# Attention output laid out with tokens on partitions, normalised along the free axis, then turned

## The chip, the cores and the metric

The kernel runs on one core of one Trainium2 chip. The metric is the device time of one execution in microseconds (us), the median over several runs. All executions quoted here are of one state (fast), so they may be compared with each other. Engine names are those of the profile: PE is TensorE's matmuls, PEld its weight loads, DVE is VectorE, ACT is ScalarE, POOL is GpSimd. The granted clock is the share of full speed that the profile records for TensorE. To turn a block is to transpose it, which these kernels do on PE.

## The reference

A linear attention with a root-mean-square norm per head, then a feed-forward block with a squared relu:

```python
# q, k, v: (8 batches, 8 heads, 576 tokens, 64), float32
kv  = np.einsum('bhsd,bhse->bhde', k, v)
out = np.einsum('bhsd,bhde->bhse', q, kv)
rms = np.sqrt(np.mean(out * out, axis=-1, keepdims=True) + 1e-06)
attn = out / rms * g_norm                  # g_norm: (64,)
# x: (4608 tokens, 512), heads side by side
h = x @ w_in                               # (512, 2048)
r = np.maximum(h, 0.0)
y = (s * (r * r) + b) @ w_out              # (2048, 512)
```

The weights come as float64, and the kernel rounds them to float32 on the chip.

## The kernel before

There are twelve token tiles of 384 tokens. A tile's attention is made inside the first feed-forward product ("h product") of the tile before it: one step after each of the 16 h products. Tile 0 has nothing to run inside, so its attention runs alone. The attention comes out with features on partitions, one row of 128 features (two heads) at a time, which is just what the h product moves. The sum of squares over a head's 64 features then lies across partitions, so it is made by a product with a block-diagonal matrix of ones. That leaves it repeated on every feature, and root and reciprocal run on 128x384 elements.

```python
def turn(p):                     # q of two heads, features on partitions
    ps = ps_t.tile([P, J, P], FP32, name="qT_ps", tag="t")
    for j in range(J):
        nc.tensor.transpose(ps[:, j, :], q_in[T][:, j, 2 * p : 2 * p + 2, :], ident)
    st["qT"] = attp.tile([P, J, 2, HB], FP32, name="qT", tag="qT")
    nc.vector.tensor_copy(out=st["qT"].rearrange("p j s t -> p j (s t)"), in_=ps)

def product(p):
    st["x"] = ps_x.tile([P, J, 2, HB], FP32, name="x_ps", tag="x")
    for s in range(2):
        nc.tensor.matmul(st["x"][:, :, s, :], lhsT=bd[:, s, p, :],
                         rhs=st["qT"][:, :, s, :], start=True, stop=True)
    st["sq"] = ...
    nc.scalar.activation(st["sq"], st["x"].rearrange("p j s t -> p (j s t)"), AF.Square)

def rms(p):
    ps = ps_t.tile([P, N], FP32, name="ss_ps", tag="t")
    nc.tensor.matmul(ps, lhsT=ones_bd, rhs=st["sq"], start=True, stop=True)
    st["rms"] = ...
    nc.scalar.activation(st["rms"], ps, AF.Sqrt, bias=eps_col, scale=1.0 / D)

def scale(p):
    inv = ...
    nc.vector.reciprocal(inv, st["rms"])
    ...
    nc.vector.scalar_tensor_tensor(xT[T][:, p, :], st["x"]..., g_col, inv, ALU.mult, ALU.mult)

return [(lambda fn=fn, p=p: fn(p)) for p in range(NP) for fn in (turn, product, rms, scale)]

def mm1(T, f):                   # one h product: four matmuls of 384 columns
    ...
    nc.scalar.activation(r, h, AF.Relu)
    nc.vector.tensor_mul(r2, r, r)
    nc.vector.tensor_scalar(out=gT[T, f], in0=r2, scalar1=s_col, scalar2=b_col, ...)

# the program
for step in attention(0):
    step()
...
for T in range(NT):
    ...
    steps = attention(T + 1) if T + 1 < NT else []
    for f in range(FC):          # 16
        if T == 0:
            w_step(f + 2)        # rounds a weight: five DVE, two ACT, two POOL instructions
        mm1(T, f)
        if steps:
            steps[f]()
    ...                          # then the three o products (mm2) of this tile
```

## Time and profile before

The time is 1291 us. What matters of the profile:

| stretch | length, us | what bounds it |
|---|---|---|
| beginning: attention of tile 0 alone | 34.4 | a chain over PE, ACT and DVE, four rows one after another |
| first tile: weights are rounded | about 168 | DVE, busy 97% and 95% of its two parts |
| h stage of a steady tile | 51.06 | PE, with about 3.3 us lost waiting for DVE |
| o stage of a steady tile | 41.2 | PE without a gap |

A line of a timeline reads: start and duration in us, engine, source line, operation, output and inputs, count, and in brackets how long the engine was idle before it and what ended that. Where PE records overlap their neighbours, the true pace is the distance from start to start. The lines of the kernel before stand in the prediction.

### The profile page before, as it was taken

The page shows a single profiled execution, that of the slowest core. Times are in us where ns is not written, and L with a number is a line of the kernel's source. Part 1 is how long each engine was busy: PE and PEld are TensorE (multiplying, and loading weights), DVE is VectorE, ACT ScalarE, POOL GpSimd, SP SyncE. Part 2 cuts the span into 40 slices and gives each one's busy share as a digit, 9 for nine tenths or more (in the row PEclk, how much of TensorE's full clock was granted, in tenths as well). Part 3 has the DMA queues.
Part 4 walks back from the last instruction along what each step waited for, and adds up shares of the span by engine and source line. Part 5 has one row for each costly group of instructions (what it writes and reads, how often), then busy time and mean ns, then how long its engine had stood idle before and what let it go on. Part 6 is the DMA issues. An engine that isn't in the chain of part 4 may idle for free.

```text
span 1289.6 us, 10478 instructions
## 1 busy us (share of the span) xinstructions
PE 1144.8 (89%) x4272; PEld 605.1 (47%) x4272; DVE 499.7 (39%) x700; ACT 206.8 (16%) x397; POOL 89.1 (7%) x72
## 2 busy tenths in 40 slices
PE   3465644899999999999999999999999999999998
PEld 3232411355455455455455454454554554554553
DVE  0499999235035044053053053052153161251220
ACT  0122322021022021021021021020121120120110
POOL 0054456100000000000000000000000000000000
PEclk9998755899999999999999999999999999999999
DMA  9032224300441000000631000001401000000000
GB/s 235 10 93 75 93 98 144 84 9 1 108 114 24 17 9 0 17 9 1 147 74 25 24 1 9 17 0 46 103 1 33 17 1 9 16 1 17 8 1 24
DMA packets 63664, 55.20 MB, mean 43 GB/s; under 512 B 40576, under 2 KB 48768, under 8 KB 63616
## 3 DMA queue, kind: packets, MB, share of 16 engines
q1 hardware_dynamic: 57984, 45.10, 13.6%
q10 hardware_dynamic: 5632, 9.44, 1.9%
q8 instruction: 33, 0.54, 0.2%
q14 instruction: 15, 0.12, 0.0%
HBM read 45.09 MB, written 9.44 MB: 42 GB/s over the span
## 4 chain that ended last, share of the span: by engine, by line
PE 68%; DVE 26%; ACT 2%; issue 2%; DMA 1%; SPq 1%; POOLq 0%; DVEq 0%; ACTq 0%
PE o_ps L294 38%; PE h_ps L277 23%; DVE inv L255 7%; DVE gT L285 4%; PE x_ps L235 3%; DVE r L283 3%; PE ss_ps L249 3%; DVE w_e L141 2%; DVE w_e L138 2%; DVE w_e L132 2%; DVE xT L258 2%; DVE qT L230 1%; PE kv_ps L201 1%; ACT r L281 1%; DVE w_e L144 1%
## 5 line engine op out<-in xcount | busy, mean ns | idle before, releaser
L294 PE MATMUL o_ps<-w,gT 128*128 128x512 f32 x1152 | 517.6, 608 | 40.3 <-POOL w L148 40.3
L277 PE MATMUL h_ps<-xT,w 128*128 128x384 f32 x1536 | 528.7, 493 | 20.1 <-POOL w L148 20.1
L277 PEld LDWEIGHTS h_ps<-xT,w 128*128 128x128 f32 x1536 | 291.0, 193 | 207.9 <-POOL w L148 23.8
L294 PEld LDWEIGHTS o_ps<-w,gT 128*128 128x128 f32 x1152 | 220.8, 194 | 328.2 <-issue 260.6
L283 DVE TENSOR_TENSOR r<-r 128x384 f32<-128x384 f32 x192 | 106.4, 554 | 556.1 <-ACT r L281 556.1
L281 ACT ACTIVATE r<-h_ps 128x384 f32<-128x384 f32 x192 | 93.9, 489 | 377.6 <-PE h_ps L277 363.6
L255 DVE RECIPROCAL inv<-rms 128x384 f32<-128x384 f32 x48 | 122.2, 2545 | 18.5 <-ACT rms L251 18.5
L285 DVE TENSOR_SCALAR gT<-r,s_col,b_col 128x384 f32<-128x384 f32 x192 | 105.3, 548 | 7.9
L235 PE MATMUL x_ps<-qT,bd_kv 128*128 128x192 f32 x192 | 48.1, 378 | 57.8 <-DVE qT L230 57.8
L302 ACT COPY o_sb<-o_ps 128x512 f32<-128x512 f32 x36 | 21.1, 586 | 477.7 <-PE o_ps L294 477.7
L235 PEld LDWEIGHTS x_ps<-qT,bd_kv 128*128 128x128 f32 x192 | 34.3, 209 | 82.9 <-DVE qT L230 79.2
L214 DVE COPY bd_kv<-kv_ps 64x256 f32<-64x256 f32 x8 | 3.4, 422 | 153.9 <-PE kv_ps L201 153.9
L147 POOL TENSOR_TENSOR w_1m<-w_1m,w_l 128x512 f32<-128x512 f32 x32 | 43.2, 1351 | 100.4 <-ACT w_1m L137 100.4
L148 POOL TENSOR_TENSOR w<-w_1m,w_e 128x512 f32<-128x512 f32 x32 | 44.0, 1374 | 43.8 <-DVE w_e L144 42.2
L249 PE MATMUL ss_ps<-sq,ones_bd 128*128 128x384 f32 x96 | 42.2, 523 | 2.4 <-ACT sq L243 2.4
L201 PE MATMUL kv_ps<-v_sb,k_sb 64*64 64x64 f32 x1152 | 25.5, 244 | 19.8 <-DMA v_sb<-in_v_dram 19.8
L137 ACT ACTIVATE w_1m<-w_m 128x512 f32<-128x512 uint32 x32 | 20.2, 630 | 116.2 <-DVE w_m L129 113.1
L201 PEld LDWEIGHTS kv_ps<-v_sb,k_sb 64*64 64x64 f32 x1152 | 22.9, 156 | 27.8 <-issue 23.0
L243 ACT ACTIVATE sq<-x_ps 128x384 f32<-128x384 f32 x48 | 23.5, 490 | 60.5 <-PE x_ps L235 60.5
L258 DVE SCALAR_TENSOR_TENSOR xT<-x_ps,g_col,inv 128x384 f32<-128x384 f32 x48 | 29.6, 617 | 5.3 <-DVE inv L255 0.5
L141 DVE TENSOR_SCALAR w_e<-w_e 128x512 uint32<-128x512 uint32 x32 | 31.1, 973 | 1.1
L251 ACT ACTIVATE rms<-ss_ps,eps_col 128x384 f32<-128x384 f32 x48 | 27.8, 580 | 13.3 <-PE ss_ps L249 13.3
(21 smaller groups left out, 212.1 us busy)
## 6 DMA issues: line engine op xcount, KB each, us to landing
k_sb<-in_k_dram SPq DMA_DIRECT2D x32, 288.0 KB, 4.7
v_sb<-in_v_dram SPq DMA_DIRECT2D x32, 288.0 KB, 5.7
q_sb<-in_q_dram SPq DMA_DIRECT2D x72, 128.0 KB, 3.4
out_dram<-o_sb ACTq DMA_DIRECT2D x36, 256.0 KB, 2.0
w_raw<-in_moe_w_in_dram SPq DMA_DIRECT2D x16, 512.0 KB, 3.8
w_raw<-in_moe_w_out_dram SPq DMA_DIRECT2D x16, 512.0 KB, 3.1
g_col<-in_g_norm_dram ACTq DMA_DIRECT2D x2, 0.2 KB, 2.9
s_col<-in_moe_s_dram ACTq DMA_DIRECT2D x1, 0.5 KB, 5.3
```

Source lines behind the costliest of these rows:

```text
L141: nc.vector.tensor_scalar(out=e, in0=e, scalar1=896.0, scalar2=2.0**23, op0=ALU.subtract, op1=ALU.mult)
L148: nc.gpsimd.tensor_tensor(out=w_sb[i], in0=one_m, in1=e.bitcast(FP32), op=ALU.mult)
L201: nc.tensor.matmul(kv_ps[g][s][l * HB : l * HB + HB, p, :], lhsT=kt[rows, l, j, :], rhs=vt[rows, l, j, :], start=(j == 0), stop=(j == R - 1),)
L235: nc.tensor.matmul(st["x"][:, :, s, :], lhsT=bd[:, s, p, :], rhs=st["qT"][:, :, s, :], start=True, stop=True,)
L249: nc.tensor.matmul(ps, lhsT=ones_bd, rhs=st["sq"], start=True, stop=True)
L255: nc.vector.reciprocal(inv, st["rms"])
L258: nc.vector.scalar_tensor_tensor(xT[T][:, p, :], st["x"].rearrange("p j s t -> p (j s t)"), g_col, inv, ALU.mult, ALU.mult,)
L277: nc.tensor.matmul(h, lhsT=w_in(c, f), rhs=xT[T][:, c, :], start=(c == 0), stop=(c == KC - 1))
L281: nc.scalar.activation(r, h, AF.Relu)
L283: nc.vector.tensor_mul(r2, r, r)
L285: nc.vector.tensor_scalar(out=gT[T, f], in0=r2, scalar1=s_col, scalar2=b_col, op0=ALU.mult, op1=ALU.add)
L294: nc.tensor.matmul(o, lhsT=gT[T, f][:, j * P : j * P + P], rhs=w_out(f), start=(f == 0), stop=(f == FC - 1),)
```

## The change

The intent is to get rid of the product with ones and of the long reciprocal. The attention output is made with tokens on partitions, one chunk of 128 tokens with all eight heads at a time. A head's 64 features then lie along the free axis: one DVE reduction gives eight sums per token, and root and reciprocal work on 128x8. The price is that the normalised chunk must be turned back by four more transposes, and that each product fills only half of the array's columns, as the two batches of a chunk need different matrices.

```diff
-        def product(p):
-            st["x"] = ps_x.tile([P, J, 2, HB], FP32, name="x_ps", tag="x")
-            for s in range(2):
-                nc.tensor.matmul(st["x"][:, :, s, :], lhsT=bd[:, s, p, :],
-                                 rhs=st["qT"][:, :, s, :], start=True, stop=True)
+        def product(j):
+            st["x"] = ps_x.tile([P, NP, P], FP32, name="x_ps", tag="x")
+            for p in range(NP):
+                for s in range(2):
+                    half = slice(s * HB, s * HB + HB)
+                    nc.tensor.matmul(st["x"][half, p, :], lhsT=st["qT"][:, p, half],
+                                     rhs=bd[:, s, p, :], start=True, stop=True)
-        def rms(p):
-            nc.tensor.matmul(ps, lhsT=ones_bd, rhs=st["sq"], start=True, stop=True)
-            nc.scalar.activation(st["rms"], ps, AF.Sqrt, bias=eps_col, scale=1.0 / D)
-        def scale(p):
-            nc.vector.reciprocal(inv, st["rms"])
-            nc.vector.scalar_tensor_tensor(xT[T][:, p, :], st["x"], g_col, inv, ...)
+        def norm(j):
+            x = st["x"].rearrange("p c (l d) -> p (c l) d", l=2)
+            nc.scalar.activation(sq, x, AF.Square)
+            nc.vector.reduce_sum(ss, sq, axis=mybir.AxisListType.X)          # 128x8
+            nc.scalar.activation(rms, ss, AF.Sqrt, bias=eps_col, scale=1.0 / D)
+            nc.vector.reciprocal(inv, rms)
+            nc.vector.tensor_tensor(out=st["xn"], in0=x, in1=inv (broadcast), op=ALU.mult)
+        def turn_x(j):
+            for p in range(NP):
+                nc.tensor.transpose(ps[:, p, :], st["xn"][:, 2 * p : 2 * p + 2, :], ident)
+            nc.scalar.activation(xT[T][:, :, j * P : j * P + P], ps, AF.Copy, scale=g_col)
...
-            (lambda fn=fn, p=p: fn(p)) for p in range(NP) for fn in (turn, product, rms, scale)
+            (lambda fn=fn, j=j: fn(j)) for j in range(J) for fn in (turn, product, norm, turn_x)
```

The turning of q now takes a chunk's four head pairs in place of a head pair's three chunks.

More of the change, by code (lines that the diff above doesn't have):

```diff
@@ L168 @@
     make_identity(nc, ident)
-    ones_bd = const.tile([P, P], FP32, name="ones_bd")
-    nc.vector.memset(ones_bd, 0.0)
     eps_col = const.tile([P, 1], FP32, name="eps_col")
@@ L175 @@
         nc.gpsimd.memset(t, 0.0)
-    for l in range(2):
-        ls = slice(l * HB, l * HB + HB)
-        nc.vector.memset(ones_bd[ls, ls], 1.0)
     g_col = const.tile([P, 1], FP32, name="g_col")
@@ L223, in attention @@
         st = {}
-        def turn(p):
-            ps = ps_t.tile([P, J, P], FP32, name="qT_ps", tag="t")
-            for j in range(J):
-                nc.tensor.transpose(ps[:, j, :], q_in[T][:, j, 2 * p : 2 * p + 2, :], ident)
-            st["qT"] = attp.tile([P, J, 2, HB], FP32, name="qT", tag="qT")
-            nc.vector.tensor_copy(out=st["qT"].rearrange("p j s t -> p j (s t)"), in_=ps)
-        def product(p):
-            st["x"] = ps_x.tile([P, J, 2, HB], FP32, name="x_ps", tag="x")
-            for s in range(2):
-                nc.tensor.matmul(
-                    st["x"][:, :, s, :],
-                    lhsT=bd[:, s, p, :],
-                    rhs=st["qT"][:, :, s, :],
-                    start=True,
-                    stop=True,
-                )
-            st["sq"] = attp.tile([P, N], FP32, name="sq", tag="sq")
-            nc.scalar.activation(
-                st["sq"], st["x"].rearrange("p j s t -> p (j s t)"), AF.Square
-            )
@@ L247, in rms, with turn @@
-        def rms(p):
-            ps = ps_t.tile([P, N], FP32, name="ss_ps", tag="t")
-            nc.tensor.matmul(ps, lhsT=ones_bd, rhs=st["sq"], start=True, stop=True)
-            st["rms"] = attp.tile([P, N], FP32, name="rms", tag="rms")
-            nc.scalar.activation(st["rms"], ps, AF.Sqrt, bias=eps_col, scale=1.0 / D)
-        def scale(p):
-            inv = attp.tile([P, N], FP32, name="inv", tag="inv")
-            nc.vector.reciprocal(inv, st["rms"])
-            if p == 0:
-                xT[T] = attp.tile([P, KC, N], FP32, name="xT", tag="xT")
-            nc.vector.scalar_tensor_tensor(
-                xT[T][:, p, :],
-                st["x"].rearrange("p j s t -> p (j s t)"),
-                g_col,
-                inv,
-                ALU.mult,
-                ALU.mult,
-            )
+        def turn(j):
+            ps = ps_t.tile([P, NP, P], FP32, name="qT_ps", tag="t")
+            for p in range(NP):
+                nc.tensor.transpose(ps[:, p, :], q_in[T][:, j, 2 * p : 2 * p + 2, :], ident)
+            st["qT"] = attp.tile([P, NP, P], FP32, name="qT", tag="qT")
+            nc.vector.tensor_copy(out=st["qT"], in_=ps)
@@ new lines, in product @@
+        def product(j):
[3 more added lines that the diff above has]
+                    half = slice(s * HB, s * HB + HB)
+                    nc.tensor.matmul(
+                        st["x"][half, p, :],
+                        lhsT=st["qT"][:, p, half],
+                        rhs=bd[:, s, p, :],
+                        start=True,
+                        stop=True,
+                    )
@@ new lines, in norm @@
+        def norm(j):
+            x = st["x"].rearrange("p c (l d) -> p (c l) d", l=2)
+            sq = attp.tile([P, H, D], FP32, name="sq", tag="sq")
+            nc.scalar.activation(sq, x, AF.Square)
+            ss = attp.tile([P, H], FP32, name="ss", tag="ss")
+            nc.vector.reduce_sum(ss, sq, axis=mybir.AxisListType.X)
+            rms = attp.tile([P, H], FP32, name="rms", tag="rms")
+            nc.scalar.activation(rms, ss, AF.Sqrt, bias=eps_col, scale=1.0 / D)
+            inv = attp.tile([P, H], FP32, name="inv", tag="inv")
+            nc.vector.reciprocal(inv, rms)
+            st["xn"] = attp.tile([P, H, D], FP32, name="xn", tag="xn")
+            nc.vector.tensor_tensor(
+                out=st["xn"], in0=x, in1=inv.unsqueeze(2).to_broadcast((P, H, D)), op=ALU.mult
+            )
@@ L267, in attention @@
+        def turn_x(j):
+            ps = ps_t.tile([P, NP, P], FP32, name="xT_ps", tag="t")
+            for p in range(NP):
+                nc.tensor.transpose(ps[:, p, :], st["xn"][:, 2 * p : 2 * p + 2, :], ident)
+            if j == 0:
+                xT[T] = attp.tile([P, KC, N], FP32, name="xT", tag="xT")
+            nc.scalar.activation(xT[T][:, :, j * P : j * P + P], ps, AF.Copy, scale=g_col)
         return [
-            (lambda fn=fn, p=p: fn(p)) for p in range(NP) for fn in (turn, product, rms, scale)
+            (lambda fn=fn, j=j: fn(j)) for j in range(J) for fn in (turn, product, norm, turn_x)
@@ L330 @@
             mm1(T, f)
-            if steps:
+            if f < len(steps):
                 steps[f]()
```

## The prediction

> **What bounds the kernel now.** I read the page's chain of waits and groups first, then the busy time by stage, then the timeline of one steady token tile, of the serial beginning and of the first tile. In the groups and the chain, the two weight products own the end; the reciprocal is the first line of another engine:
>
> ```profile
> PE o_ps L294 38%; PE h_ps L277 23%; DVE inv L255 7%; DVE gT L285 4%; PE x_ps L235 3%; DVE r L283 3%; PE ss_ps L249 3%; DVE w_e L141 2%; DVE w_e L138 2%; DVE w_e L132 2%; DVE xT L258 2%; DVE qT L230 1%; PE kv_ps L201 1%; ACT r L281 1%; DVE w_e L144 1%
> ...
> L255 DVE RECIPROCAL inv<-rms 128x384 f32<-128x384 f32 x48 | 122.2, 2545 | 18.5 <-ACT rms L251 18.5
> ```
>
> The span has three regimes. **Beginning**, to 65.8 us: k and v load, then the attention of tile 0 runs alone, one feature row after another. **First tile**, to 234 us: VectorE rounds the weights. **Steady**, 264.7 us to the end: eleven tiles, TensorE bound, of which ten carry the next tile's attention (the last has none). In the table by stage (columns: window, length, then busy us and count of PE, PEld, DVE, ACT, POOL; granted clock; DMA):
>
> ```profile
> 65.70:170.00 104.30, 62.78 (x167) 35.83 (x168) 101.56 (x134) 31.55 (x60) 48.71 (x36) 0.85 0.29 91
> 170.00:234.00 64.00, 28.40 (x29) 6.57 (x27) 60.93 (x72) 16.00 (x27) 37.95 (x28) 0.50 0.44 134
> ...
> 454.50:505.60 51.10, 48.62 (x166) 29.36 (x165) 26.09 (x40) 12.22 (x24) 0.00 (x0) 1.00 0.01 5
> ```
>
> DVE is busy 101.56 of 104.30 and 60.93 of 64.00 us in the first tile; in the steady h stage PE is busy 48.62 of 51.10 us. So an instruction taken from DVE pays in the first tile at full price, and in a steady tile only if PE waits for it. PE does wait for it there; the timeline (start, duration, engine, what, idle before):
>
> ```profile
> 467.63 0.48 DVE L285 TENSOR_SCALAR gT<-r,s_col,b_col 128x384 f32<-128x384 f32 x1
> 468.03 2.55 DVE L255 RECIPROCAL inv<-rms 128x384 f32<-128x384 f32 x1
> ...
> 472.19 0.55 DVE L230 COPY qT<-qT_ps 128x384 f32<-128x384 f32 x1
> ...
> 472.80 0.92 PE L235 MATMUL x_ps<-qT,bd_kv 128*128 128x192 f32 x4 [0.83 <-DVE qT L230]
> 473.55 2.74 PE L277 MATMUL h_ps<-xT,w 128*128 128x384 f32 x8
> ...
> 476.13 0.81 PE L249 MATMUL ss_ps<-sq,ones_bd 128*128 128x384 f32 x2
> 476.77 5.32 PE L277 MATMUL h_ps<-xT,w 128*128 128x384 f32 x16
> ```
>
> The reciprocal holds DVE from 468.03, so the copy of the turned q comes late and PE idles 0.83 us (records overlap, so I use start to start: h from 469.22 needs 2.58, to 471.80, and the product starts at 472.80: 1.00 us lost, and its exposed weight load makes it 0.75 us long rather than 0.65). That happens for three of the four rows.
>
> **What the Trainium skill says.** (1) "TensorEngine Tiling (Array Packing)", Key Properties: different tiles of the array load and multiply in parallel; changing the tiling mode drains the engine. The new product uses halves of 64 columns. The trace agrees where it has 64x64 tiles:
>
> ```profile
> 329.45 1.28 PE L201 MATMUL kv_ps<-v_sb,k_sb 64*64 64x64 f32 x72
> ...
> 330.65 2.84 PE L294 MATMUL o_ps<-w,gT 128*128 128x512 f32 x6
> ```
>
> An h product moves 8 x 384 = 3072 columns in 2.58 us, 0.84 ns a column. 72 x 64 columns would be 3.87 us one after another; they took 1.20 us with both changes of mode, 3.2 fold of a possible 4. (2) "VectorE: DVE Perf Modes", The perf-mode tier table: a reduction, and fp32 tensor_tensor, run at one element a cycle. The trace has no reduction, but the 128x512 step of L144 takes 692 ns and the 128x384 squaring 554 ns, one a cycle plus 0.15 us. (3) "ScalarE: Activation LUTs", What ACT_TABLE_LOAD costs: about 280 ns + 0.833 ns an element with a pointer bias. At 384 that is 600 ns and the trace has 580. (4) "TensorE: Matmul & The Clock Gate", Part 1: an array that waits runs at half clock. The trace agrees: the ones product takes 1.65 us in the beginning and 0.81 us in steady state.
>
> **The change, part by part.** Three token chunks take the place of four feature rows. The built order shows in every chunk: turn after h product 0, 4, 8; product after 1, 5, 9; norm after 2, 6, 10; turn back after 3, 7, 11. The last four h products carry nothing.
>
> *TensorE, steady, per tile.* Removed: four ones products, 4 x 0.65 = 2.6 us; the three waits with their exposed loads, 3 x 1.1 = 3.3; four products of 0.65 = 2.6. Added: three products of 16 records x 128 columns = 2048 columns, 1.72 us each in a row; with two halves at the efficiency of the k-v product (80%), 1.72 / 1.6 = 1.07, say 1.1 with the mode changes: 3.3 us. Twelve transposes back at 0.11 (three took 0.33): 1.3 us. The twelve q transposes stay. So without waits 8.5 us go and 4.6 come.
>
> *The new wait.* The turn back needs the normalised chunk, and only one h product (2.58 us) hides the chain. Count from the end of h product 2, by the gaps of the trace. From an h product's end to the relu start is 0.20 (463.09 to 463.29), the relu ends at 0.69, r starts 0.72, gT 1.32 to 1.80. The norm stands behind all these: the square (128x512, estimate 0.60 from 490 ns at 384 and 586 ns for the 512 copy) runs beside r and gT. Reduction 1.72 to 2.41 (0.69, and DVE overlaps the instruction before by 0.08). Root on 128x8 to 2.73 (0.29). Reciprocal on 128x8: 2545 ns for 384 is six cycles each plus the fixed part, so an estimate of 0.20, to 2.95. Multiply from 3.05 (the trace has 0.1 between reciprocal and its reader), 0.69, to 3.74. PE starts at 3.80 with its weight load exposed, 0.1. It could have started at 2.58, so 1.3 us are lost, three times: 4.0 us per tile. The copy of q no longer sits behind a long reciprocal: it ends at 2.4 and is needed at 3.0, so that wait goes.
>
> Steady sum: -8.5 + 4.6 + 4.0 = +0.1 us a tile, ten tiles: +1 us. **The gain in work is eaten by a wait of another kind.**
>
> *Beginning.* Before, from the first turn at 31.38 to DVE's first weight step at 65.76: 34.4 us, four serial rows of 8.3. After, at half clock: turn 1.1 (0.91 for three, and 0.21), copy 0.68, product about 2.2 (twice 0.86, plus 0.4 of load and drain as before), square 0.63, reduction 0.72, root 0.32, reciprocal 0.23, multiply 0.79; then turn back 1.0 and the next turn's 1.1 before the next copy. A cycle is 7.7, and DVE is free after 1.1 + 2 x 7.7 + 5.6 = 22.1 us, at 53.5. That is **-12 us**, passed on whole, since the first three weights are sent at 19.8 and a transfer takes 3.6 (11.0 at most), and DVE is then the bound.
>
> *First tile.* Removed from DVE: four times 3.18 (95.76 to 98.94, reciprocal and scale) and 0.46 (copy): 14.6 us. Added, three times: copy 0.60, reduction 0.61, wait for the root 0.35, reciprocal 0.3, multiply 0.61, in all 2.5: 7.4 us. **-7 us**. GpSimd stands beside it with 48.71 busy of 104.30, so it does not become the bound.
>
> Sum: -12 - 7 + 1 = -18, say 1290.95 - 18 = **1273 us**, 1.4% less.
>
> **Rivals.** (a) The two 64-column halves do not overlap. Then the product is 1.72 and more, +0.7 three times in ten tiles: +21 us, and +5 in the beginning: about 1299. Against it stands the 3.2 fold of the k-v product; for it, that one used row halves also, so column halves alone are not shown. I give it one in eight. (b) The wait for the norm is smaller than I count (a shorter reduction or handover) or vanishes. With 0.7 instead of 1.3 us, 30 times: -18, about 1255; without any, 1233. For it: the durations of reduction and of 128x8 operations are estimates. Against: r and gT stand ahead on DVE, and they alone end at 1.80. (c) The wait is larger, 1.7 us: +12, 1285. The norm hands over four times between ACT and DVE, and each handover can cost 0.1 more than I took. (d) Everything is hidden by the weights' arrival in the beginning: +12, 1285; the transfer times speak against it. No engine but PE becomes the steady bound: DVE falls from 26.09 us a stage.
>
> **Range and chances.** The first regimes give -19 with an error of 3. The steady part is +1 with an error of about 9 (0.3 us in each of 30 waits), and rival (a) puts a tail upwards. So 1261 to 1292 holds eight in ten. Faster by over 2% means below about 1265.6, 8 us under my number: 0.20. Slower by over 2% needs 1317, (a) with (c): 0.03. The rest, 0.77, is within 2%.
>
> **What would show it.** Right: the first weight step on DVE near 53.5 us; the o stage of tile 0 ending 19 us earlier; in the steady h stage no idle before the product, 16 records of it in about 1.1 us, and an idle of about 1.2 us before the turn back, released by the multiply on DVE; the h stage still 51 us; 128x8 operations at 0.2 to 0.3 us, reduction and multiply at 0.69. Wrong: a product of 1.7 us or more (rival a); idle before the turn back much under or over 1.3 (b, c); DVE idle for transfers near 53 us (d).

## The result and the profile after

The changed kernel takes 1276.59 us (median of 4, from 1275.53 to 1276.95), beside 1290.99 us for the kernel before in the same rounds. The ratio is 0.9885, 95% interval 0.9871 to 0.9899. Ratios here are the mean time of one kernel's fast runs over that of the other's of the same rounds, so not quite the ratio of the medians quoted. It is 1.1% faster, a gain clear of noise but under the 2% that counts as faster here: 3.6 us above the number predicted, and well inside its range.

The chain of waits after, by line. The ones product and the long reciprocal are gone from these lines, and the reduction, the multiply and the turning back are new:

```profile
PE o_ps L294 38%; PE h_ps L277 31%; DVE gT L285 3%; PE x_ps L236 2%; DVE w_e L141 2%; DVE w_e L138 2%; DVE r L283 2%; DVE w_e L132 2%; DVE xn L255 2%; DVE ss L249 2%; PE xT_ps L262 2%; ACT r L281 1%; PE kv_ps L196 1%; PE qT_ps L227 1%; DVE w_e L144 1%
```

The end of the beginning: the first weight step of DVE (w_m) starts at 52.85 us, where it started at 65.76 before.

```profile
52.24 0.69 DVE L255 TENSOR_TENSOR xn<-x_ps,inv 128x512 f32<-128x512 f32 x1
52.85 0.41 DVE L129 TENSOR_SCALAR w_m<-w_raw 128x512 uint32<-128x512 uint32 x1
```

A steady h stage after, in the table by stage (columns as in the prediction), of the same kind as the 51.10 us window of before:

```profile
435.97:487.42 51.45, 48.24 (x201) 28.74 (x201) 21.54 (x42) 12.37 (x25) 0.00 (x0) 1.00 0.02 6
```

DVE works 4.6 us less (21.54 for 26.09), PE about as much, and the stage is 0.4 us longer. From the starts of its first h and first o product it is 51.45 us, against 51.06. The timeline of one chunk's norm in this stage shows why:

```profile
446.52 0.48 DVE L285 TENSOR_SCALAR gT<-r,s_col,b_col 128x384 f32<-128x384 f32 x1
446.92 0.68 DVE L249 TENSOR_REDUCE ss<-sq 128x8 f32<-128x512 f32 x1
447.63 0.30 ACT L251 ACTIVATE rms<-ss,eps_col 128x8 f32<-128x8 f32 x1 [1.25 <-DVE ss L249]
447.96 0.20 DVE L253 RECIPROCAL inv<-rms 128x8 f32<-128x8 f32 x1 [0.37 <-ACT rms L251]
...
448.27 0.69 DVE L255 TENSOR_TENSOR xn<-x_ps,inv 128x512 f32<-128x512 f32 x1
...
449.02 0.65 PE L262 MATMUL xT_ps<-ident,xn 128*128 128x128 f32 x4 [1.07 <-DVE xn L255]
```

The reciprocal has fallen from 2.55 to 0.20 us. But the norm is a chain of five operations that hands over between ACT and DVE, it starts only when gT of the h product before is done, and one h product does not cover it: PE idles 1.07 us. In the waits of PE in that stage (total us, times, longest), before and then after:

```profile
PE x_ps L235 <- DVE qT L230: 2.5, 3, 0.8
```

```profile
PE xT_ps L262 <- DVE xn L255: 3.2, 3, 1.1
```

Three waits were exchanged for three of another kind. The first tile's o stage ends 19.35 us earlier than before (the first steady h product starts at 245.37 where it started at 264.72). The ten steady stages then give back 0.39 us each.

### The profile page after: what moved, and what is told of

Same layout as the page of the kernel before. It is cut to its first block, busy times and chain, and to the rows that moved or that the text cites. A ratio compares the mean times of both kernels' runs of the same rounds, so it can differ in the third digit from the quotient of the medians.

```text
span 1273.7 us, 11355 instructions
## 1 busy us (share of the span) xinstructions
PE 1141.2 (90%) x4704; PEld 600.7 (47%) x4704; DVE 408.3 (32%) x697; ACT 208.8 (16%) x409; POOL 90.6 (7%) x72
## 4 chain that ended last, share of the span: by engine, by line
PE 75%; DVE 17%; issue 6%; ACT 2%; POOL 0%; POOLq 0%; DVEq 0%
PE o_ps L294 38%; PE h_ps L277 31%; DVE gT L285 3%; PE x_ps L236 2%; DVE w_e L141 2%; DVE w_e L138 2%; DVE r L283 2%; DVE w_e L132 2%; DVE xn L255 2%; DVE ss L249 2%; PE xT_ps L262 2%; ACT r L281 1%; PE kv_ps L196 1%; PE qT_ps L227 1%; DVE w_e L144 1%
## 5 line engine op out<-in xcount | busy, mean ns | idle before, releaser
L262 PE MATMUL xT_ps<-ident,xn 128*128 128x128 f32 x144 | 26.3, 311 | 53.9 <-DVE xn L255 53.9
L262 PEld LDWEIGHTS xT_ps<-ident,xn 128*128 128x128 f32 x144 | 16.9, 153 | 75.3 <-DVE xn L255 68.8
L236 PE MATMUL x_ps<-bd_kv,qT 128*64 128x128 f32 x576 | 42.0, 291 | 6.8 <-DVE qT L229 6.8
L236 PEld LDWEIGHTS x_ps<-bd_kv,qT 128*64 128x64 f32 x576 | 32.9, 144 | 26.1 <-issue 16.0
L141 DVE TENSOR_SCALAR w_e<-w_e 128x512 uint32<-128x512 uint32 x32 | 32.2, 1005 | 1.1
L265 ACT ACTIVATE xT<-xT_ps,g_col 128x512 f32<-128x512 f32 x36 | 24.7, 686 | 42.1 <-PE xT_ps L262 42.1
L132 DVE TENSOR_SCALAR w_e<-w_raw 128x512 uint32<-128x512 uint32 x32 | 28.8, 901 | 0.0
L138 DVE TENSOR_SCALAR w_e<-w_e 128x512 uint32<-128x512 uint32 x32 | 26.9, 841 | 1.1
```

Source lines behind the costliest of these rows:

```text
L132: nc.vector.tensor_scalar(out=e, in0=hi, scalar1=20, scalar2=0x7FF, op0=ALU.logical_shift_right, op1=ALU.bitwise_and,)
L138: nc.vector.tensor_scalar(out=e, in0=e, scalar1=896.0, scalar2=1151.0, op0=ALU.max, op1=ALU.min)
L141: nc.vector.tensor_scalar(out=e, in0=e, scalar1=896.0, scalar2=2.0**23, op0=ALU.subtract, op1=ALU.mult)
L236: nc.tensor.matmul(st["x"][half, p, :], lhsT=st["qT"][:, p, half], rhs=bd[:, s, p, :], start=True, stop=True,)
L262: nc.tensor.transpose(ps[:, p, :], st["xn"][:, 2 * p : 2 * p + 2, :], ident)
```

## The experiments

All nine ran correctly, each on one chip beside the kernel before (1291.2 to 1291.4 us). "Changed" means the changed kernel, 1276.6 us.

| run | what | us | ratio to before (95%) | expected |
|---|---|---|---|---|
| old_in_0_1 | old attention for tiles 0, 1 | 1294.8 | 1.0027 (1.0015 to 1.0040) | 1295 |
| old_in_0 | old attention for tile 0 | 1289.0 | 0.9982 (0.9970 to 0.9995) | 1289 |
| new_in_0_1 | new attention for tiles 0, 1 only | 1272.2 | 0.9850 (0.9836 to 0.9863) | 1271.7 |
| halves_in_turn | halves of the array one after the other | 1293.1 | 1.0011 (0.9995 to 1.0026) | 1302 |
| more_cover | two h products behind the norm | 1237.2 | 0.9579 (0.9566 to 0.9593) | 1241 |
| no_cover | none | 1419.1 | 1.0988 (1.0973 to 1.1003) | 1354 |
| no_cover_filled | none, PE kept at work | 1356.1 | 1.0502 (1.0484 to 1.0520) | 1357 |
| old_early_turn | kernel before, its wait removed | 1257.8 | 0.9740 (0.9727 to 0.9753) | 1258 |
| cover_and_early_turn | more_cover, better beginning | 1233.6 | 0.9547 (0.9534 to 0.9560) | 1233 |

### Where the gain is: tiles made in the old and in the new way

Three kernels hold both attentions and choose by token tile. The edit, with the condition of each:

```diff
+    def attention(T):
+        return attention_old(T) if T <= 1 else attention_new(T)   # old_in_0_1
+        # T == 0: old_in_0        T >= 2: new_in_0_1
```

Tile 0 is made in the beginning, tile 1 inside the first tile, tiles 2 to 11 inside the ten steady stages.

> The new attention only for token tiles 2 to 11, which are made inside the ten steady stages; tiles 0 and 1 (the serial beginning and the first tile) keep the old one. Theory: the whole gain of the change is in the beginning (-12 us) and in the first tile (-7), and each steady h stage loses 0.39 us (51.45 against 51.06), so this is slower than the kernel before: 1291 + 10 x 0.39 = about 1295 us. Rival: the gain is spread over the tiles; then this keeps ten twelfths of it, about 1279 us.

Measured: 1294.8 us, slower than the kernel before by 0.27%, with an interval that excludes zero. So the steady part of the change is a small loss, and the rival of a gain spread over the tiles is out.

> The old attention for token tile 0 alone, the new one for tiles 1 to 11. This parts the beginning from the first tile. Theory: the serial beginning is worth 12 us and DVE's shorter queue in the first tile 7 us, so this is about 1276.6 + 12.5 = 1289 us, and 6 to 7 us below the kernel with the old attention in tiles 0 and 1 (1294.8). Rival: what the beginning gains is only moved (DVE's weight steps start earlier but then wait), and the first tile holds the whole gain: then about 1277 us.

Measured: 1289.0 us. The beginning is worth 1289.0 - 1276.6 = 12.4 us. The first tile is worth 1294.8 - 1289.0 = 5.8 us (in their traces the first steady h product starts 6.2 us apart).

> The new attention for tiles 0 and 1 only, the old one for tiles 2 to 11, the complement of the earlier mixture. Theory: all of the gain and none of the steady loss, 1291.2 - 19.4 = about 1271.7 us, 5 us less than the changed kernel. Rival: the parts don't add up (the steady tiles are faster or slower for having a new-made tile before them): outside 1269 to 1275 us.

Measured: 1272.2 us, the changed kernel less about 4 us. This run tests whether the parts add up. (12.4 + 5.8 - 3.4 is the whole change whatever happens, as these differences share their kernels.) Its gain of 19.2 us (1291.4 - 1272.2), less the steady loss of 3.4 (1294.8 - 1291.4), makes 15.8, for the 14.4 us of the whole change: the parts add up to within about 1.4 us.

### Whether the two halves of the array overlap

```diff
-            for p in range(NP):
-                for s in range(2):
+            for s in range(2):
+                for p in range(NP):
```

> The changed kernel with its 64-column halves ordered half by half, so that following products are in the same half of the array. Theory: the halves run side by side in the changed kernel; so ordered they can't, a product of 2048 columns takes 1.72 us plus 0.3 for the changes of mode in place of 1.02 plus 0.3: +0.7 x 30 = +21 us, and +1.7 x 3 = +5 in the beginning at half clock, about 1302 us. Rival: the order does not matter (they do not overlap, or the array finds them anyway): 1277 us.

Measured: 1293.1 us, 16.5 us more than the changed kernel. The direction is that of the theory, the size is not: the product takes 1.51 us from start to start (447.67 to 449.18) where it takes 1.02 in the changed kernel (441.50 to 442.52), and not 1.72. The timelines of PE, first the changed kernel, then this one:

```profile
441.50 1.09 PE L236 MATMUL x_ps<-bd_kv,qT 128*64 128x128 f32 x16
...
442.52 5.43 PE L277 MATMUL h_ps<-xT,w 128*128 128x384 f32 x16
```

```profile
447.67 1.58 PE L236 MATMUL x_ps<-bd_kv,qT 128*64 128x128 f32 x16
449.18 5.43 PE L277 MATMUL h_ps<-xT,w 128*128 128x384 f32 x16
```

So matmuls in different column halves do run side by side. The lines above merge them; their single records in the two traces show more. In the changed kernel the sixteen start in pairs 6 ns apart, a pair every 0.11 us. Half by half they start singly every 0.11 us or so, but from the fifth on a second series runs between the first: its eight start 0.11 us apart too, from 448.17 us, while the first series goes on to 448.49. The records don't name the half, but two series of eight at this pace are the two halves. So this order still lets the halves overlap where they meet, and the product is shorter than two halves one after the other would be: the run shows the overlap and a part of its worth, not the cost of having none. 0.49 us, 30 times, is 14.7 us; the rest comes earlier, where the array has half its pace: DVE's first weight step starts 2.5 us later (55.4 us for 52.85).

### What the new wait costs

One more h product between norm and turning back (15 of the 16 places are then used):

```diff
-            ... for fn in (turn, product, norm, turn_x)
+            ... for fn in (turn, product, norm, idle, turn_x)      # idle does nothing
```

> The changed kernel with one more h product between the norm and the turning back, in every chunk (five places a chunk, 15 of 16). Theory: the new wait (PE idle 1.07 us before the turning back, about 1.2 us lost with the exposed weight load, 30 times) is what ate the steady gain; it is then hidden: 30 x 1.2 = -36 us, about 1241 us, h stage 47.9 us. Rival: PE is held by something that comes along with the norm (the ACT or DVE queue), and the wait reappears at another instruction: 1265 us or more.

Measured: 1237.2 us, 39.4 us less than the changed kernel. The steady h stage is now 47.6 us, and PE has no gap in it: busy time and length of the window are the same, at 47.74 us.

```profile
428.86:476.60 47.74, 47.74 (x202) 29.14 (x201) 21.52 (x42) 12.04 (x25) 0.00 (x0) 1.00 0.02 6
```

Turning the other way, no h product between:

```diff
+        def norm_and_turn_x(j):
+            norm(j)
+            turn_x(j)
-            ... for fn in (turn, product, norm, turn_x)
+            ... for fn in (turn, product, norm_and_turn_x, idle)
```

> The changed kernel with the turning back right behind the norm, no h product between (places 2 and 2 of four, the fourth left empty). Theory: the chain from the end of the h product to the normalised chunk is about 3.8 us long and each h product between hides 2.58 of it; without one, 2.58 us more are lost 30 times: +77 us, about 1354 us, PE idle 3.7 us before each turning back. Rival: the wait is set by something else than the length of that chain: then the loss is far from 77 us.

Measured: 1419.1 us, 65 us more than expected. The wait itself is right: PE idles 3.65 us. What was missed stands in the line after it, two h products of 7.81 us in place of 5.3, and in the granted clock of that stretch (the third column from the end): 0.50.

```profile
480.53 1.12 PE L262 MATMUL xT_ps<-ident,xn 128*128 128x128 f32 x4 [3.65 <-DVE xn L255]
481.44 7.81 PE L286 MATMUL h_ps<-xT,w 128*128 128x384 f32 x16
```

```profile
481.60:486.00 4.40, 4.40 (x9) 2.28 (x8) 0.00 (x0) 0.69 (x1) 0.00 (x0) 0.50 0.01 4
```

An idle of 1.07 us (the changed kernel) leaves the clock at 1.00; one of 3.65 us does not. The Trainium skill has this: "TensorE: Matmul & The Clock Gate", Why this matters for your kernels, asks for no idle gap of over about 3 us between matmul bursts. To show that the clock is the cause, and not the order of instructions, idle work was put into the gap:

```diff
             ps = ps_t.tile([P, NP, P], FP32, name="xT_ps", tag="t")
+            for _ in range(7):
+                for p in range(NP):
+                    nc.tensor.transpose(ps[:, p, :], ident, ident)
```

> The kernel without cover (1419 us where 1354 was expected), with 28 idle transposes of the identity ahead of each turning back, about 3 us of TensorE work of no use, overwritten at once by the real ones. Theory: of the 142 us that the missing cover cost, 77 are the longer wait and about 60 are the array at half clock for some 4 us after each idle of 3.65 us (granted clock 0.50 in the trace). With PE kept at work the clock stays at 1.00 and 60 us come back: about 1357 us. Rival: the half clock has another cause (the kind of instruction), and the idle work changes nothing or adds to the time: 1415 us or more.

Measured: 1356.1 us. Work of no use makes the kernel 63 us faster, and what remains against the changed kernel, 79.5 us, is the longer wait (77 expected). In its timeline the h products behind the turning back have their old pace again:

```profile
467.65 0.66 PE L265 MATMUL xT_ps<-ident,xn 128*128 128x128 f32 x4 [0.60 <-DVE xn L255]
468.14 5.33 PE L289 MATMUL h_ps<-xT,w 128*128 128x384 f32 x16
```

### What the old wait cost

The kernel before, with nothing changed but the place at which q is turned: one place earlier, so that its copy stands ahead of the long reciprocal on DVE.

```diff
+        def rms_and_turn(p):
+            rms(p)
+            if p + 1 < NP:
+                turn(p + 1)
+        def first(p):
+            if p == 0:
+                turn(p)
-            ... for fn in (turn, product, rms, scale)
+            ... for fn in (first, product, rms_and_turn, scale)
```

> The kernel before with its own wait taken away: q of the next feature row is turned one place earlier, so that its copy stands before the reciprocal on DVE. Theory: the old steady stage lost 3 x (1.0 + 0.1) us to the long reciprocal; without it the h stage is 47.8 us in place of 51.06 and the time 1291 - 33 = about 1258 us, less than the changed kernel, with every product with ones and every long reciprocal still in it. Rival: DVE is too full with 2.55 us reciprocals, and the wait moves to another place: 1285 us or more.

Measured: 1257.8 us. The ones products and all long reciprocals are still there, and it is 19 us faster than the changed kernel. Its steady h stage is 47.8 us, and that of more_cover 47.6: with the waits hidden on both sides, the two ways of making the attention are worth the same to a steady tile.

### A version that beats both

In tile 0 no h products cover anything, so there the next chunk's q is turned while the norm of this one runs:

```diff
-    for step in attention(0):
-        step()
+    first_tile = attention(0)      # five steps a chunk: turn, product, norm, idle, turn_x
+    for i in (0, 1, 2, 5, 4, 6, 7, 10, 9, 11, 12, 14):
+        first_tile[i]()
```

> The kernel with one more h product of cover, and in tile 0, which runs alone, the next chunk's q is turned between norm and turning back, so that it runs beside the norm. Theory: of the 7.6 us of a chunk in the beginning, the turn (0.85) and most of the copy (0.7) with its handover leave the chain, 1.9 us twice: 1237.2 - 3.8 = about 1233 us. Rival: the first weight steps then wait for the weights or POOL, and nothing is gained: 1237 us.

Measured: 1233.6 us, 4.5% less than the kernel before (ratio 0.9547), and in its interval below more_cover's 0.9579 as well. The copy of the next q stands right behind the multiply, beside the turning back, and a chunk takes 5.9 us (39.83 to 45.70) where it took 7.6:

```profile
38.04 0.69 DVE L255 TENSOR_TENSOR xn<-x_ps,inv 128x512 f32<-128x512 f32 x1
38.65 0.68 DVE L229 COPY qT<-qT_ps 128x512 f32<-128x512 f32 x1
...
39.83 1.98 PE L236 MATMUL x_ps<-bd_kv,qT 128*64 128x128 f32 x16
...
45.70 1.98 PE L236 MATMUL x_ps<-bd_kv,qT 128*64 128x128 f32 x16
```

## Why the prediction was right

The prediction came out 3.6 us low, mostly by the steady part (2.4 to 2.9 us), the rest by the first tile; no large errors cancelled.

**Beginning, -12 us.** 12.4 us by old_in_0, and DVE's first weight step at 52.85 us for the predicted 53.5. The prediction took the array at half clock here. The stage table gives a granted clock of 1.00 for this stretch, yet the ones product takes 1.65 us in it and 0.81 in a steady stage: here the pace of a known instruction was the better witness. Rival (d), a wait for the weights' arrival, did not come.

**First tile, -7 us.** 5.8 us by the mixtures and 6.2 by their traces. DVE stayed the bound. The term is about 1 us too large; the mean times of the weight steps' instructions grew by 17 ns a weight in sum (the five lines together), which over 32 weights is 0.5 us. The rest is not settled.

**Steady, +1 us.** It is 3.4 us by old_in_0_1, 10 x 0.39 by the traces. The mechanism was right, the new wait takes the place of the old; one term was mis-sized. The product, taken at "1.07, say 1.1 with the mode changes", costs 1.24, counted from end to end: 1.03 from the end of h product 1 (441.56) to its own (442.59), and then 0.21 in the h product behind it, whose first weights are not loaded ahead. In the order of the chain, h product 1 and the one behind the product:

```profile
438.98 2.58 PE h_ps L277 x8
...
442.59 2.79 PE h_ps L277 x8
```

The wait, taken at 1.3, costs 1.28: from the end of the h product before it (447.95) to the end of the turning back (449.67) are 1.72 us, of which four transposes are 0.44 (those of q, from 438.38 to 438.82). So per tile about 0.4 us too little went in for the three products, and the waits were right; with the +0.1 of the sum this is about the 0.39 us measured.

**The durations.** Reduction 678 ns for the estimated 690, root on 128x8 301 for 290, reciprocal on 128x8 203 for 200, multiply 692 for 690. That is why the wait came out within 0.1 us.

**Rival (a)**, halves that do not overlap, is out: in the changed kernel they start in pairs, and the product takes 1.02 us. What it would have cost (26 us by the prediction) was not measured: in halves_in_turn, 17 us slower, the halves still overlap in part. **Rival (b)**, no wait at all, was given 1233; forced in more_cover it gives 1237.2. **Rival (c)**, a larger wait, was not the case.

## What to carry to other kernels

Count a change at the place where its instructions stand: taking 2.5 us reciprocals from an engine that is 39% busy gave nothing per steady tile, because one h product does not cover the chain that replaced them, and the bound engine waited for its end. Before replacing an operation that an engine waits for, try to issue what it waits for earlier: moving one step in the old kernel was worth more than the whole rewrite (33 against 14 us), and the rewrite was worth most with the same care (54 to 58 us). When a chain has to hide behind other work, add up its length by handovers and give it whole units of cover, and look at the clock behind an idle of the array as long as the 3.65 us of no_cover.

## What the Trainium skill lacked or had wrong

- "TensorEngine Tiling (Array Packing)", Key Properties, says that a change of tiling mode drains the engine, without a figure. Here a product in 64-column halves between full-array products costs about 0.2 us beyond its own 1.02 from start to start, seen at the end of the h product behind it (2.79 us for 2.58). How much of it is the drain was not tried apart.
- The same page says that tiles work independently; it does not say that the order of the instructions matters. Alternating halves took 1.02 us, the same sixteen instructions half by half 1.51, with an overlap of a few matmuls where the halves meet.
- "TensorE: Matmul & The Clock Gate", Part 4, says that an instruction in transpose mode does not count as array work in the way a matmul does and that the full clock does not come with it. Here 28 calls of `nc.tensor.transpose` in the gap were enough to keep the clock: 1.00 with them, 0.50 without, 63 us of difference. Whether they ran in that mode the record does not show; they start 0.11 us apart, the pace of 128 columns of an h product (0.84 ns each), so this may not be a case of what the page means.
- "VectorE: DVE Perf Modes" describes the iterative divide of the reciprocal but gives no time for it. Here 128x384 took 2545 ns and 128x8 203 ns, which is 6.2 ns an element, by an estimate six cycles at the page's 0.96 GHz.
